# Runs of four channels instead of two in the spectra buffers of a long convolution

## Chip, cores and metric

The kernel runs on one core of a Trainium2 chip. The time is that of the device for one execution, in microseconds (us); lower is better.

## The reference

The input `u` has 2048 positions of 640 channels. Two branches work on it and a gate mixes them for each position:

```python
g = sigmoid((x * gate_w).sum(-1, keepdims=True))
# branch A: a state space layer as a long convolution, for each channel
K = 2.0 * einsum("dn,dnl->dl", C, exp(A * dt * pos)).real        # 640 x 2048 taps
y = irfft(rfft(u_t, 4096) * rfft(K, 4096), 4096)[..., :2048]     # causal convolution
a = y.T + u * D_skip
# branch B: feed-forward, 640 -> 1728 -> 640
b = maximum(x @ w1, 0) @ w2
out = g * a + (1 - g) * b
```

## The kernel before

The kernel has three kinds of work. The taps of the convolution are generated from the parameters in the first 405 us or so (tiles `pg`, `px`, `pk`, `sc`, `mg`, `G`, `kt`). The feed-forward branch goes through the hidden dimension in three passes of 5, 5 and 4 slices and keeps the partial sums in DRAM (tiles `pf`, `xx`, `w1h`, `w1l`, `w2h`, `w2l`, `hh`, `hl`, `q`). The convolution itself, in `conv`, runs from about 409 us, beside the third feed-forward pass, whose matmuls fill TensorE between its own.

The convolution is done by Fourier transforms in two factors, as matmuls with tables, for five blocks `i` of 128 channels. For each block:

1. `stage1`: the kernel's taps (`ck`) and the signal (`xu`) are multiplied with the table `tf` into a PSUM tile `pc`; each of four steps `q` covers 32 channels. VectorE then transposes the tile in blocks of 32x32 (`turn`, two instructions for a tile) into the spectra buffer `ku`. The output is addressed by `blocks`.
2. `stage2`: for each of eight groups `j` of four frequencies, matmuls with the table `tm` read kernel and signal spectra of one frequency for all 128 channels from `ku` (one moving operand of 2x128 columns). ScalarE copies one product from PSUM to `ku` (`copy`), VectorE makes two complex products (`mul`, into `kx` and into `ku`), and GpSimd adds and subtracts (`add`).
3. `inv2`: matmuls with the table `tn` read `ku`, again one frequency and 128 channels at a time; ScalarE copies the sums back (`back`).
4. `relay`: VectorE transposes eight pieces from the one half of `ku` to the other.
5. `inv1`: matmuls with `tw` read four frequencies of 128 channels (512 columns); ScalarE scales by the gate into `yo`, and the result goes out, or to a sum with the other branch.

One `ku` buffer holds, for each partition, kernel and signal spectra: 2 x 32 frequencies x 128 channels in float32. There are two such buffers. Within a half, channel `d` and frequency `g` lie at element 64·(d div 2) + 2·g + (d mod 2): channels in runs of two, and the frequencies of such a pair side by side.

The PSUM tiles `pc` come from a ring of three, and TensorE's queue is executed in order. The order of all instructions is made when the program is built: each step is a task with an engine, a duration estimate, a rank and the buffers it takes (`Plan.add`), and `Plan.run` lists the tasks by modelled due times. All engine calls go through one helper, so that the profile shows them all at line 408; they are told apart by their tiles.

Of the kernel before, what the change touches and what calls it, by code (L numbers as in the profile page):

```python
# [429 lines left out]
class Kernel:  # L430
# [850 lines left out]
    def conv(self, C=128):  # L1281
# [7 lines left out]
        st = {}  # L1289
# [8 lines left out]
        def table(k, shape, src):  # L1298
            def go():
                st[k] = self.pr.tile(shape, F32, name=k)  # L1300
                D_.dma_start(st[k], io[src])
            return A('SP', 'tab', 0.62, go, [opened], kb=math.prod(shape) * 4 / 1024, rank=3)
# [30 lines left out]


        def blocks(x, d0):
            return x[:, :, d0 // 2:d0 // 2 + 8].rearrange("p g e f -> p e f g")

        def stage1(kind, i, q, src):
            s_, ld = src
            b_ = tok('psc')  # L1340
            k = kind == 'k'
            if k and q == 0:
                K[i] = tok('K')
            buf = K[i]

            def pe():
                x = st['ck', i, q] if k else st['cu', i]
                p = st['p1', kind, i, q] = self.psc.tile([128, 2, 512], F32, name="pc")
                for c in range(2):
                    for h in range(2):  # L1350
                        r, o, d = slice(h * 64, h * 64 + 64), slice(c * 64, c * 64 + 64), slice(q * 32, q * 32 + 32)
                        self.E.matmul(p[o, h], st['tf'][r, int(k), o], x[r] if k else x[r, :, d], start=True, stop=True)

            def turn(h):
                def go():
                    if k and q == 0 and h == 0:
                        t = self.pr.tile([128, 2, 32, C], F32, name="ku", bufs=2)
                        st['ku', i] = t.rearrange("p k a b -> p k (a b)").rearrange("p k (e g f) -> p k g e f", g=32, f=2)
                        st['K', i], st['U', i] = st['ku', i][:, 0], st['ku', i][:, 1]
                    p = st['p1', kind, i, q]  # L1360
                    if k:
                        pv, d0 = p[:, h].rearrange("p (d b) -> p d b", b=32), h * 64 + q * 16
                    else:
                        pv, d0 = p.rearrange("p h (b d) -> p d h b", d=32)[:, 16 * h:16 * h + 16], q * 32 + h * 16
                    V.transpose(out=blocks(st['K' if k else 'U', i], d0), in_=pv)
                return go
            new = k and q == 0
            a = A('PE', 's' + kind, 0.87, pe, [ld, tf, opened] + ([] if k else [first[i]]), take=[b_, buf] if new else [b_], use=[s_] if new else [s_, buf],
                  rank=SKR if k else SUR, mode='c')
            pes[kind, i, q] = a  # L1370
            if JS1 and q % 2:
                self.plan.join([pes[kind, i, q - 1], a])
            ts = [A('DVE', 's' + kind, 0.68, turn(h), [a], use=[b_, buf], rank=SKD if k else SUD)
                  for h in range(2)]
            if new:
                first[i] = ts[0]
            return ts
# [3 lines left out]
        def stage2(i, j, dep):  # L1381
            b_, x_ = tok('psc'), tok('kx')

            def pe():
                ps = self.psc.tile([128, 2, 4, C], F32, name="pc")
                for a in range(2):
                    for m in range(4):
                        for p in range(2):
                            r, g = slice(p * 64, p * 64 + 64), 4 * j + m
                            self.E.matmul(ps[32 * m:32 * m + 32, p, 2 * a:2 * a + 2].rearrange("q k (e f) -> q k e f", f=2),  # L1390
                                          st['tm'][r, g, 32 * a:32 * a + 32], st['ku', i][r, :, g], start=True, stop=True)
                st['p2', i, j] = ps.rearrange("q p (a k) (e f) -> q k a p e f", a=2, f=2)

            def copy():
                S.copy(whole(i, j), st['p2', i, j][:, 0])

            def mul(a):
                def go():
                    k = whole(i, j)
                    if a:  # L1400
                        st['kx', i, j] = self.pr.tile([128, 2, 2, C], F32, name="kx", bufs=KX).rearrange(
                            "q b p (e f) -> q b p e f", f=2)
                    V.tensor_mul(st['kx', i, j] if a else k,
                                 st['p2', i, j][:, 1, None, a].to_broadcast([128, 2, 2, C // 2, 2]), k)
                return go

            def add(k):
                def go():
                    y, x = whole(i, j)[:, k], st['kx', i, j][:, 1 - k]
                    (P.tensor_add if k else P.tensor_sub)(y, y, x)  # L1410
                return go
            f = A('PE', None, 0.92, pe, dep, take=[b_], use=[K[i]], rank=S2P, mode='c', n=32)
            c = [A('ACT', 's2', 0.52, copy, [f], use=[b_, K[i]], rank=0.5)]
            for a in (1, 0):
                c.append(A('DVE', 's2', 0.62, mul(a), c, take=[x_] if a else (), use=[b_, K[i]] + [x_] * (1 - a), rank=S2D))
            return f, [A('POOL', 's2', 0.7, add(k), c, use=[x_, K[i]], rank=1) for k in range(2)]


        def whole(i, j):
            return st['K', i][:, 4 * j:4 * j + 4].rearrange("q (b p) e f -> q b p e f", b=2)  # L1420


        def inv2(i, h, dep):
            bs = tok('psc'), tok('psc')

            def pe(gs):
                if 0 in gs:
                    st['p3', i, h] = [self.psc.tile([128, 2, 4, C], F32, name="pc") for _ in range(2)]
                px = st['p3', i, h]
                for g in gs:  # L1430
                    for q in range(2):
                        for m in range(4):
                            for p in range(2):
                                r = slice(32 * m, 32 * m + 32)
                                self.E.matmul(px[m // 2][p * 64:p * 64 + 64, m % 2, g].rearrange("q (e f) -> q e f", f=2),
                                              st['tn'][r, 4 * h + g, p, q],
                                              whole(i, 4 * h + g)[r, q, p], start=q == 0, stop=q == 1)

            def back(k):
                def go():  # L1440
                    S.copy(st['U', i][:, 16 * h:16 * h + 16].rearrange("q (g m) e f -> q m g e f", m=4)[:, 2 * k:2 * k + 2],
                           st['p3', i, h][k].rearrange("q m g (e f) -> q m g e f", f=2))
                return go
            vs = []
            for t in range(TURNS):
                gs = range(t * 4 // TURNS, (t + 1) * 4 // TURNS)
                vs.append(A('PE', None, 1.85 / TURNS, lambda gs=gs: pe(gs), [*dep, tn] + vs[-1:], take=() if t else bs,
                            use=[K[i]] + (list(bs) if t else []), rank=S2P, mode='c', n=128 // TURNS))
            v = vs[-1]
            return vs, [A('ACT', 's2', 0.96, back(k), [v], use=[bs[k], K[i]], rank=0) for k in range(2)]  # L1450


        def relay(i, r, dep):
            return A('DVE', 'rl', 0.7, lambda: V.transpose(out=blocks(st['K', i], r * 16), in_=blocks(st['U', i], r * 16)),
                     dep, use=[K[i]], rank=RLR)
# [4 lines left out]
        def inv1(i, j, dep):  # L1460
            last = i == n - 1
            for q in range(2):
# [8 lines left out]
                def pe(q=q, b0=b0):  # L1471
                    py = st['p4', i, b0] = self.psc.tile([128, 2, 4, C], F32, name="pc")
                    for h in range(2):
                        self.E.matmul(py[h * 64:h * 64 + 64, 0].rearrange("q b (e f) -> q b e f", f=2), st['tw'],
                                      st['K', i][:, h * 16 + b0:h * 16 + b0 + 4], start=True, stop=True)

                def copy(q=q, b0=b0, ns=ns, y_=y_, first=first):
# [7 lines left out]
                a = A('PE', 's4', 0.87, pe, [*dep, tw], take=[b_], use=[K[i]], rank=S4R, mode='c1')  # L1485
# [49 lines left out]
        tm, tw, tn = table('tm', [128, 32, 64], 't_m'), table('tw', [128, 64], 't_w'), table('tn', [128, 8, 2, 2, 64], 't_n')  # L1535
# [69 lines left out]
```

## Time and profile before

| | us |
|---|---|
| median of 3 runs | 658.9 (657.89 to 659.11) |
| profiled execution | 659.89 |
| its span | 658.1 |

The mean granted TensorE clock of the profiled execution was 0.991 of full speed. In the lines of the profile PE is TensorE's matmul, PEld its weight load, DVE is VectorE, ACT ScalarE, POOL GpSimd, SP the queue of DMA issues. In a line of the tile view, the three numbers are minimum, median and maximum of one instruction in ns. In the lines of the timeline, the first two numbers are start and length in us, and the bracket holds the idle time of the engine before it and what ended it. In the view by stretches, the columns are the stretch, its length, the busy time of the engine (number of instructions), the granted clock, the share of DMA and GB/s. A matmul in float32 appears as two records with the same shape, so that `x1280` are 640 matmuls of the program.

### The profile page before, as it was taken

Reading aid. Unit: us, or ns where it says so; the run is one execution under the profiler, and the core shown is the slowest. Engines: PE = TensorE matmul, PEld = TensorE weight load, DVE = VectorE, ACT = ScalarE, POOL = GpSimd, SP = SyncE. Lnnn points to the kernel's source line nnn. Section 1 sums busy time; section 2 is a strip of 40 time slices with the busy share of each in tenths; the row PEclk is TensorE's granted clock in tenths of the full one; section 3 lists DMA queues with packets and bytes.
Section 4 is the critical chain, followed back from the end, with each engine's and each line's share of the span. In section 5 each row is a group of like instructions: output and inputs, shape, how many; then the busy total and the mean of one; then the engine's idle time right before and its main releaser. Section 6 shows DMA issues by size and latency. Waiting matters only on the chain. (4 is left out here: it accounts for less than half of the span.)

```text
span 658.1 us, 19202 instructions
## 1 busy us (share of the span) xinstructions
PE 637.3 (97%) x8236; PEld 509.0 (77%) x8236; DVE 510.2 (78%) x778; ACT 404.0 (61%) x603; POOL 96.6 (15%) x133
## 2 busy tenths in 40 slices
PE   7999999999999999999999999998997989999996
PEld 6999999899978988988988987645574445476576
DVE  4899838989999989999999995675677647685442
ACT  5467459998999888789889780051442343413531
POOL 0000000000000000000000000060430632712741
PEclk9999999999999999999999999999899999999999
DMA  9946855324575334432532359935417665264635
GB/s 262 316 186 196 271 146 167 108 74 154 147 233 174 121 116 152 153 113 79 207 124 77 97 151 297 287 89 117 145 56 212 123 177 107 49 227 141 181 90 129
DMA packets 76302, 102.79 MB, mean 156 GB/s; under 512 B 7609, under 2 KB 59449, under 8 KB 75962
## 3 DMA queue, kind: packets, MB, share of 16 engines
q1 hardware_dynamic: 76058, 101.16, 51.0%
q8 instruction: 65, 1.06, 0.7%
q10 hardware_dynamic: 160, 0.41, 0.3%
q14 instruction: 19, 0.16, 0.1%
HBM read 62.36 MB, written 39.19 MB: 154 GB/s over the span
## 5 line engine op out<-in xcount | busy, mean ns | idle before, releaser
L408 PE MATMUL pf<-xx,w1h 128*128 128x256 f32 (+1 forms) x760 | 187.4, 343 | 0.8 <-issue 0.4
L408 PEld LDWEIGHTS pf<-xx,w1h 128*128 128x128 f32 x760 | 125.7, 191 | 33.3 <-issue 18.9
L408 PE MATMUL pf<-xx,w1l 128*128 128x512 f32 (+1 forms) x340 | 116.6, 343 | 0.0
L408 ACT COPY ku<-pc 128x512 f32<-128x512 f32 (+1 forms) x60 | 44.5, 760 | 81.9 <-PE pc L408 81.7
L408 PE MATMUL pf<-w2h,hh 128*128 128x320 f32 x288 | 89.9, 316 | 0.4 <-ACT hh L408 0.4
L408 PE MATMUL pf<-w2l,hh 128*128 128x320 f32 x288 | 87.9, 309 | 0.0
L408 PE MATMUL pf<-w2h,hl 128*128 128x320 f32 x256 | 73.6, 313 | 0.0
L408 PEld LDWEIGHTS pf<-xx,w1l 128*128 128x128 f32 x340 | 65.0, 191 | 7.7 <-DVE w1l L408 0.2
L408 POOL TENSOR_TENSOR ku<-ku,kx 128x256 f32<-128x256 f32 x80 | 59.3, 776 | 65.2 <-PE pc L408 56.3
L408 DVE STREAM_TRANSPOSE ku<-pc 128x512 f32<-128x512 f32 x80 | 51.0, 689 | 22.8 <-PE pc L408 22.4
L408 POOL TENSOR_TENSOR kt<-kt,dsk 128x8 f32<-128x8 f32 x20 | 9.6, 480 | 392.0 <-DVE kt L408 275.5
L408 PEld LDWEIGHTS pf<-w2h,hh 128*128 128x128 f32 x288 | 54.2, 188 | 7.7 <-issue 6.2
L408 ACT ACTIVATE hh<-pf 128x512 fp32r<-128x512 f32 (+1 forms) x40 | 20.4, 510 | 57.7 <-PE pf L408 57.7
L408 PEld LDWEIGHTS pf<-w2l,hh 128*128 128x128 f32 x288 | 54.3, 188 | 0.6
L408 DVE TENSOR_TENSOR sc<-pg,sc 128x1024 f32<-128x1024 f32 x40 | 48.7, 1218 | 7.4 <-ACT sc L408 7.2
L408 ACT ACT_TABLE_LOAD x42 | 53.9, 1283 | 0.8
L408 ACT CAST sc<-pg 128x1024 int32<-128x1024 f32 x40 | 40.4, 1011 | 21.0 <-PE pg L408 20.9
L408 PE MATMUL pc<-ku,tm 64*32 64x256 f32 x1280 | 50.9, 456 | 0.2 <-DVE ku L408 0.2
L408 PEld LDWEIGHTS pf<-w2h,hl 128*128 128x128 f32 x256 | 46.5, 188 | 5.2 <-issue 4.6
L408 DVE TENSOR_TENSOR mg<-mg,sc 128x1024 f32<-128x1024 f32 x40 | 48.9, 1222 | 1.5
L408 DVE TENSOR_TENSOR sc<-sc,me 128x1024 f32<-128x1024 f32 x40 | 48.7, 1217 | 0.0
L408 ACT ACTIVATE sc<-sc,half_pi 128x1024 f32<-128x1024 f32 x40 | 45.7, 1142 | 0.0
(168 smaller groups left out, 1249.8 us busy)
## 6 DMA issues: line engine op xcount, KB each, us to landing
xx<-xt SPq DMA_DIRECT2D x24, 640.0 KB, 5.8
xt<-xx SPq DMA_DIRECT2D x16, 640.0 KB, 3.6
part<-q SPq DMA_DIRECT2D x16, 640.0 KB, 3.4
q<-part SPq DMA_DIRECT2D x16, 640.0 KB, 4.9
ws<-in_B_w_dram SPq DMA_DIRECT2D x20, 320.0 KB, 4.7
kd<-kt SPq DMA_DIRECT2D x80, 64.0 KB, 2.2
ck<-kd SPq DMA_DIRECT2D x40, 128.0 KB, 2.8
xu<-in_A_u_dram SPq DMA_DIRECT2D x10, 512.0 KB, 6.4
```

What stands on the lines that cost most here:

```text
L408: return lambda *a, **k: self._tc.keep_in_program_order(f(*a, **k))
```

## The change

The spectra buffer gets another layout: channel `d` and frequency `g` now lie at element 128·(d div 4) + 4·g + (d mod 4). Runs of four channels lie side by side, and behind them those of the next frequency. All views of the buffer are changed to it; the PSUM tiles keep their layout, since there only the names of the dimensions change. The tables, the DMAs and the number of instructions stay as they are, and so does the order in which the instructions stand on each engine. What changes in an instruction are its strides: a matmul that read 64 runs of two floats, 256 bytes apart, reads 32 runs of four, 512 bytes apart; a transpose that wrote the 32 frequencies of a channel in steps of 8 bytes writes them in steps of 16 bytes.

```diff
         def blocks(x, d0):
-            return x[:, :, d0 // 2:d0 // 2 + 8].rearrange("p g e f -> p e f g")
+            return x[:, :, d0 // 4:d0 // 4 + 4].rearrange("p g e f -> p e f g")
...
-                        st['ku', i] = t.rearrange("p k a b -> p k (a b)").rearrange("p k (e g f) -> p k g e f", g=32, f=2)
+                        st['ku', i] = t.rearrange("p k a b -> p k (a b)").rearrange("p k (e g f) -> p k g e f", g=32, f=4)
...
-                            self.E.matmul(ps[32 * m:32 * m + 32, p, 2 * a:2 * a + 2].rearrange("q k (e f) -> q k e f", f=2),
+                            self.E.matmul(ps[32 * m:32 * m + 32, p, 2 * a:2 * a + 2].rearrange("q k (e f) -> q k e f", f=4),
                                           st['tm'][r, g, 32 * a:32 * a + 32], st['ku', i][r, :, g], start=True, stop=True)
-                st['p2', i, j] = ps.rearrange("q p (a k) (e f) -> q k a p e f", a=2, f=2)
+                st['p2', i, j] = ps.rearrange("q p (a k) (e f) -> q k a p e f", a=2, f=4)
...
                         st['kx', i, j] = self.pr.tile([128, 2, 2, C], F32, name="kx", bufs=KX).rearrange(
-                            "q b p (e f) -> q b p e f", f=2)
+                            "q b p (e f) -> q b p e f", f=4)
                     V.tensor_mul(st['kx', i, j] if a else k,
-                                 st['p2', i, j][:, 1, None, a].to_broadcast([128, 2, 2, C // 2, 2]), k)
+                                 st['p2', i, j][:, 1, None, a].to_broadcast([128, 2, 2, C // 4, 4]), k)
```

In the same way `f=2` becomes `f=4` in the views of the matmuls of `inv2` and `inv1` and of the copy `back`.

More of the change, by code (lines that the diff above doesn't have):

```diff
@@ L1434, in pe @@
                                 r = slice(32 * m, 32 * m + 32)
-                                self.E.matmul(px[m // 2][p * 64:p * 64 + 64, m % 2, g].rearrange("q (e f) -> q e f", f=2),
+                                self.E.matmul(px[m // 2][p * 64:p * 64 + 64, m % 2, g].rearrange("q (e f) -> q e f", f=4),
                                               st['tn'][r, 4 * h + g, p, q],
@@ L1441, in go @@
                     S.copy(st['U', i][:, 16 * h:16 * h + 16].rearrange("q (g m) e f -> q m g e f", m=4)[:, 2 * k:2 * k + 2],
-                           st['p3', i, h][k].rearrange("q m g (e f) -> q m g e f", f=2))
+                           st['p3', i, h][k].rearrange("q m g (e f) -> q m g e f", f=4))
                 return go
@@ L1473, in pe @@
                     for h in range(2):
-                        self.E.matmul(py[h * 64:h * 64 + 64, 0].rearrange("q b (e f) -> q b e f", f=2), st['tw'],
+                        self.E.matmul(py[h * 64:h * 64 + 64, 0].rearrange("q b (e f) -> q b e f", f=4), st['tw'],
                                       st['K', i][:, h * 16 + b0:h * 16 + b0 + 4], start=True, stop=True)
```

## The prediction

> **What bounds the kernel now.** I read the page's busy times first, then the matmuls and vector operations that touch the spectra buffer, then the convolution stage in order of time.
>
> ```profile
> PE 637.3 (97%) x8236; PEld 509.0 (77%) x8236; DVE 510.2 (78%) x778; ACT 404.0 (61%) x603; POOL 96.6 (15%) x133
> PE 17%; DMA 2%; ACT 1%; SPq 1%; DVE 1%; issue 1%; POOL 0%; POOLq 0%; DVEq 0%; ACTq 0%
> ```
>
> TensorE is busy for 97% of the span, and it carries nearly all of the chain that ended last. VectorE comes second with 78%. The change touches only the operations on the buffer `ku`, which the view of that tile gives as minimum, median and maximum of one instruction:
>
> ```profile
> L408 PE MATMUL pc<-ku,tm x1280: 435/451/632, 428.2 to 614.9; 64*32 64x256 f32 x183
> L408 PE MATMUL pc<-ku,tn x1280: 265/307/466, 453.6 to 625.9; 32*64 32x128 f32 x183
> L408 DVE STREAM_TRANSPOSE ku<-pc x80: 666/678/740, 410.2 to 594.8; 128x512 f32<-128x512 f32 x80
> L408 PE MATMUL pc<-ku,tw x80: 589/591/1116, 486.3 to 638.3; 128*64 128x512 f32 x80
> L408 DVE TENSOR_TENSOR kx<-pc,ku x40: 669/687/699, 430.4 to 616.5; 128x512 f32<-128x512 f32 x40
> L408 DVE TENSOR_TENSOR ku<-pc,ku x40: 683/697/847, 431.1 to 617.2; 128x512 f32<-128x512 f32 x40
> L408 DVE STREAM_TRANSPOSE ku<-ku x40: 657/672/823, 465.5 to 633.8; 128x512 f32<-128x512 f32 x40
> ```
>
> They lie between 410 and 638 us. The number of instructions, their order on each engine and their waits are the same before and after. So everything hangs on whether one instruction takes longer or shorter with its new addresses. Two groups of addresses change in kind.
>
> **The matmuls: runs of two floats become runs of four.** Two other groups show what a matmul costs whose moving operand lies in runs of 512 and 64:
>
> ```profile
> L408 PE MATMUL pc<-ck,tf x160: 589/589/641, 409.1 to 581.5; 64*64 64x512 f32 x160
> L408 PE MATMUL pk<-mg,sc x1280: 216/219/243, 114.9 to 401.6; 128*32 128x64 f32 x183
> ```
>
> From 64 columns (219 ns) to 512 (589 ns) a column costs 370/448 = 0.83 ns. On that line 256 columns should take 378 ns and 128 columns 272 ns. The `tm` matmuls take 451, 73 more, and the `tn` matmuls 307, 35 more: in both, about 0.55 ns for each run of two. The `tw` matmuls also read runs of two and take 591 ns, on the line. They have two tiles of the array in flight; `tm` and `tn` have eight. My reading is that eight streams together ask for new places in the buffer faster than they are served: one run of two in 256x0.83/128 + 0.57 = 2.2 ns. A run of four has 3.3 ns before its next piece is due, so the wait should go. Eight matmuls run side by side, so 1280 of a kind are 160 in a row: 160x73 = 11.7 us for `tm` and 160x35 = 5.6 us for `tn`. Bounds: no gain (it is the eight tiles, not the runs) and 17.3 us.
>
> What of it is on the path is seen in one block's stage 2:
>
> ```profile
> 558.47 0.70 DVE L408 TENSOR_TENSOR kx<-pc,ku 128x512 f32<-128x512 f32 x1 [1.50 <-ACT ku L408]
> ...
> 569.68 0.82 DVE L408 TENSOR_TENSOR ku<-pc,ku 128x512 f32<-128x512 f32 x1
> ...
> 606.62 0.69 DVE L408 TENSOR_TENSOR kx<-pc,ku 128x512 f32<-128x512 f32 x1 [2.08 <-ACT ku L408]
> ```
>
> VectorE's sixteen products of this block go from 558.47 to 570.50, 12.0 us, of which 16x0.69 = 11.0 are its own work. If TensorE gets faster here, VectorE takes over after 1.0 us of the block's 11.7/5 = 2.3. In the last block, where feed-forward matmuls stand between (606.62, with 2.08 us of idle time on VectorE before one product), all 2.3 can come through. Four blocks at up to 1.0 and one at 2.3 make 6.3 at most; I take 5 of the 11.7 us. The `tn` matmuls wait for no VectorE work while they run: all 5.6. Together 10 us, if the reading is right. The products, ScalarE's copies and GpSimd's sums keep runs within a piece of the buffer and get longer ones; a product that writes in runs of two takes 697 ns, one that writes without a gap 687, so nothing is to be won there, and I put them at nothing. They would cost 10 ns x 40 = 0.4 us if that cover were wrong.
>
> **The transposes: a step of 8 bytes becomes one of 16.** A transpose writes, for each channel, 32 frequencies one behind the other; in the buffer these stand 8 bytes apart now and 16 after. The relay (`ku<-ku`) also reads in that step. No row of this profile shows VectorE at a step of 16 bytes in the same memory, so I bound it.
>
> ```profile
> L408 DVE TENSOR_TENSOR sc<-pg,sc 128x1024 f32<-128x1024 f32 x40 | 48.7, 1218 | 7.4 <-ACT sc L408 7.2
> 424.09 1.95 PE L408 MATMUL pc<-ck,tf 64*64 64x512 f32 x16
> 425.25 2.51 DVE L408 STREAM_TRANSPOSE ku<-pc 128x512 f32<-128x512 f32 x4 [2.57 <-PE pc L408]
> ...
> 545.94 1.90 PE L408 MATMUL pc<-xu,tf 64*64 64x512 f32 x16
> ...
> 552.68 2.47 DVE L408 STREAM_TRANSPOSE ku<-pc 128x512 f32<-128x512 f32 x4
> ```
>
> From below: nothing. The four transposes at 425.25 empty the matmuls of 424.09 and read kernel spectra that lie gapless in PSUM; the four at 552.68 empty those of 545.94 and read signal spectra in steps of 128 bytes there; both kinds take 0.62 us each. From above: VectorE passes an element in (1218-687)/512 = 1.04 ns, so at 8 bytes it moves to a new pair every 2.07 ns, and the 2.2 ns of the matmuls is the price of a new piece when it is asked for too fast. No row shows SBUF serving one stream at one new piece per 1.04 ns. At 2.07 ns for each element a transpose takes 512x2.07 + 90 ns = 1.15 us, 0.53 more. I exclude a gain: 0.62 us is 512x1.04 + 90 ns, the rate of the gapless products. I take the upper end, since the rows that are nearest in kind (same buffer, same memory) are the matmuls that pay for jumps, while the free row reads PSUM.
>
> The Trainium skill (Advanced Engine Details and Errata, section SBUF Cachelines) says that an access pattern runs at full rate only when at least two accesses in a row fall into the same line of 16 bytes. By it the transposes lose and the matmuls, with two floats to a line already, gain nothing; the trace speaks against the second half, with 451 ns where 378 would be full rate.
>
> **What 0.53 us x 120 does to the end.** VectorE by stretches, busy time and instructions:
>
> ```profile
> 410.00:430.00 20.00, 12.83 (x21) 1.00 0.95 285
> 443.00:465.00 22.00, 11.09 (x19) 0.93 0.45 98
> 465.00:486.00 21.00, 17.48 (x27) 0.99 0.39 144
> 486.00:516.00 30.00, 17.52 (x30) 0.94 0.68 166
> 534.00:558.00 24.00, 16.93 (x27) 1.00 0.60 138
> 574.00:598.00 24.00, 17.70 (x29) 1.00 0.55 188
> 628.00:635.00 7.00, 6.06 (x10) 1.00 0.43 129
> ```
>
> They hold 16, 16, 8, 24, 24, 24 and 8 transposes, so 8.5, 8.5, 4.2, 12.7, 12.7, 12.7 and 4.2 us more work: 63.6. If all idle time of a stretch could take it up, 1.3, 0, 0.7, 0.2, 5.6, 6.4 and 3.3 would be left: 17.5 us. But TensorE has three PSUM buffers there, its queue is in order, and it cannot catch up. The second stretch shows how much gets through:
>
> ```profile
> 440.71 1.95 PE L408 MATMUL pc<-ck,tf 64*64 64x512 f32 x16
> 443.00 2.50 DVE L408 STREAM_TRANSPOSE ku<-pc 128x512 f32<-128x512 f32 x4
> 444.17 1.09 PE L408 MATMUL pc<-xu,tf 64*64 64x512 f32 x8
> 445.08 1.11 PE L408 MATMUL pc<-ck,tf 64*64 64x512 f32 x8
> 445.42 0.66 DVE L408 SCALAR_TENSOR_TENSOR hl<-pf,hh 128x512 fp32r<-128x512 f32 x1
> 445.94 1.11 PE L408 MATMUL pc<-xu,tf 64*64 64x512 f32 x8
> 445.99 7.44 DVE L408 STREAM_TRANSPOSE ku<-pc 128x512 f32<-128x512 f32 x12
> 448.56 1.09 PE L408 MATMUL pc<-ck,tf 64*64 64x512 f32 x8
> 449.47 1.90 PE L408 MATMUL pc<-xu,tf 64*64 64x512 f32 x16
> 453.58 2.58 PE L408 MATMUL pc<-ku,tn 32*64 32x128 f32 x128
> ```
>
> Eight matmul records fill one buffer, and two transposes empty it, in 2.3 us then. From 443.0 the buffers come free at 445.3, 447.6, (after `hl`) 450.5, 452.8, 455.1, 457.4, 459.7. Each fill needs the buffer three before it: the fifth starts at 447.6 (now 445.9), the sixth at 450.5, the seventh at 452.8 (now 449.5), the eighth at 455.1. Then come 2.3 us of feed-forward, and `tn` takes two buffers, the seventh's at 459.7: 6.1 us later than now, of 8.5 added, though this stretch has 10.9 us of idle time behind the burst. So the loss lies well above the lower bound. I take the middle of 17.5 and 63.6, 40 us; the ends stay for the range. What is late next in each block is the first `tm` matmul, which needs all sixteen transposes, and `tw`, which needs all eight relays; the feed-forward matmuls queued behind them on TensorE wait too.
>
> **Sum.** The profiled execution took 659.9 us (span 658.1 and 1.8 around it), 1.0 above the median of 658.9. 659.9 + 40 - 10 = 689.9, less 1.0: **689 us**. Its own range goes from 666 (the lower bound, 17.5 us) to 704 (55 of the 63.6 lost).
>
> **Rivals.** Two per mille, 1.3 us, is about what a measurement of this kernel can tell from no change.
> - *Faster: the transposes stay at 0.62 us and the matmuls gain.* For it: 128-byte steps in PSUM are free. Against it: PSUM is not the memory written. It decides as soon as the loss per transpose is under 10/(40/0.53) = 0.13 us. 659.9 - 10 - 1 = 649 us (642 if all 17.3 come through). Chance 0.20.
> - *Only the transposes pay.* The excess of `tm` and `tn` comes from eight tiles in flight and stays; for it speaks `tw`, which reads the same runs for free. 659.9 + 40 - 1 = 699 us. Chance 0.17. This is how the page's two accesses to a line would have it.
> - *Half the price.* A transpose takes some 0.27 us more; added work 32 us, bounds 1.4 (what idle time leaves) and 32, middle 17; 17 - 10 = 7 more: 666 us. Chance 0.13.
> - *Nothing moves.* Both step and run are free: 659 us. Chance 0.08.
> The forecast, both effects, has 0.42.
>
> **Range and chances.** From 648 to 704: it leaves out the faster half-case below 648 (0.05) and the upper part of the transposes-only case and of the forecast (0.12). Faster by over 0.2%: 0.20 from the first rival and 0.02 from the half price: 0.22. Within 0.2%: 0.08. Slower: 0.70.
>
> **What would show it.** In the tile view after: `ku<-pc` and `ku<-ku` transposes near 1.15 us (right), near 0.68 (wrong, first or last rival), or between. `tm` near 378 and `tn` near 272 ns, or 451 and 307. In the waits, this line must grow to tens of us:
>
> ```profile
> PE pc L408 <- DVE ku L408: 0.2, 1, 0.2
> ```
>  If the transposes double and that idle time stays under 15 us, my coupling over three buffers is wrong.

## The result, and the profile after

The changed kernel takes 668.65 us (median of 4 runs, 667.65 to 673.05) against 659.0 before: 1.0164 times as long, 95% interval 1.0135 to 1.0192. On a second occasion it was 667.4 us, 1.0152 times (1.0129 to 1.0174). It is slower, as forecast, but by 9.7 us and not by 30. The execution that was profiled took 673.05 us (span 671.3) and is the longest of the four. So times of single instructions are read from it here, and differences of the whole from the medians.

The page's busy times after:

```profile
PE 630.2 (94%) x8236; PEld 508.0 (76%) x8236; DVE 546.6 (81%) x778; ACT 402.4 (60%) x603; POOL 92.2 (14%) x133
```

TensorE has 7.1 us less work, VectorE 36.4 us more. The view of the tile `ku` after (minimum, median, maximum of one instruction in ns) says where:

```profile
L408 PE MATMUL pc<-ku,tm x1280: 372/376/632, 431.5 to 622.8; 64*32 64x256 f32 x183
L408 PE MATMUL pc<-ku,tn x1280: 267/268/472, 458.1 to 636.4; 32*64 32x128 f32 x183
L408 DVE STREAM_TRANSPOSE ku<-pc x80: 1053/1101/1195, 410.3 to 604.7; 128x512 f32<-128x512 f32 x80
L408 POOL TENSOR_TENSOR ku<-ku,kx x80: 709/727/758, 435.0 to 628.6; 128x256 f32<-128x256 f32 x80
L408 PE MATMUL pc<-ku,tw x80: 592/592/643, 490.1 to 651.1; 128*64 128x512 f32 x80
L408 DVE TENSOR_TENSOR ku<-pc,ku x40: 681/692/694, 434.1 to 625.3; 128x512 f32<-128x512 f32 x40
L408 DVE STREAM_TRANSPOSE ku<-ku x40: 1057/1118/1206, 470.0 to 646.9; 128x512 f32<-128x512 f32 x40
```

`tm` fell from 451 to 376 ns, `tn` from 307 to 268; each transpose rose from some 675 to 1101 and 1118 ns. Both effects of the forecast are there. But the timeline of VectorE after shows that a row of transposes runs faster than single ones would suggest:

```profile
444.70 3.87 DVE L408 STREAM_TRANSPOSE ku<-pc 128x512 f32<-128x512 f32 x4
448.42 0.67 DVE L408 SCALAR_TENSOR_TENSOR hl<-pf,hh 128x512 fp32r<-128x512 f32 x1
449.01 11.20 DVE L408 STREAM_TRANSPOSE ku<-pc 128x512 f32<-128x512 f32 x12
```

Twelve in 11.20 us are 0.93 us each, where twelve took 7.44 before, 0.62 each: 0.31 us more, not 0.53. One is recorded as 1.10 us long, so the next transpose starts while the one before is still recorded as running. The waits of TensorE from 408 us on (total, times, longest, in us) have a new first line, the one named in the prediction, which had 0.2 us before:

```profile
PE pc L408 <- DVE ku L408: 17.5, 19, 3.0
PE pc L408 <- issue: 5.1, 4, 2.5
PE pc L408 <- ACT yo L408: 2.6, 2, 2.5
```

### The profile page after: what moved, and what is told of

Same layout as the page of the kernel before. It is cut to its first block, busy times and chain, and to the rows that moved or that the text cites. A ratio compares the mean times of both kernels' runs of the same rounds, so it can differ in the third digit from the quotient of the medians.

```text
span 671.3 us, 19202 instructions
## 1 busy us (share of the span) xinstructions
PE 630.2 (94%) x8236; PEld 508.0 (76%) x8236; DVE 546.6 (81%) x778; ACT 402.4 (60%) x603; POOL 92.2 (14%) x133
## 5 line engine op out<-in xcount | busy, mean ns | idle before, releaser
L408 DVE STREAM_TRANSPOSE ku<-pc 128x512 f32<-128x512 f32 x80 | 78.1, 1108 | 17.1 <-PE pc L408 17.1
L408 ACT COPY ku<-pc 128x512 f32<-128x512 f32 (+1 forms) x60 | 42.6, 730 | 79.1 <-PE pc L408 79.0
L408 POOL TENSOR_TENSOR ku<-ku,kx 128x256 f32<-128x256 f32 x80 | 55.5, 730 | 69.2 <-DVE ku L408 39.6
L408 DVE STREAM_TRANSPOSE ku<-ku 128x512 f32<-128x512 f32 x40 | 41.7, 1123 | 13.3 <-issue 9.3
```

Of the source, the lines that this page charges most:

```text
L408: return lambda *a, **k: self._tc.keep_in_program_order(f(*a, **k))
```

## The experiments

**The step of 16 bytes without long runs.** Kernel and signal spectra share one area, so that transposes step by 16 bytes and matmuls still read runs of two:

```diff
-  st['ku', i] = t.rearrange("p k a b -> p k (a b)").rearrange("p k (e g f) -> p k g e f", g=32, f=2)
+  st['ku', i] = t.rearrange("p k a b -> p (k a b)").rearrange("p (e g k f) -> p k g e f", g=32, k=2, f=2)
```

> Runs of two as before, but kernel and signal spectra share one area: element 128*(d div 2) + 4*g + 2*(kernel or signal) + (d mod 2). So the transposes step by 16 bytes, as in the changed kernel, while every matmul reads runs of two, 512 bytes apart. Theory 1 (the loss is the transposes' step, the gain the matmuls' run length): transposes 1.10 us and 0.93 back to back, tm 451 and tn 307 ns, time 659 + 20 = 679 us (672 to 684). Theory 2 (the loss is not the transposes', but the idle time of TensorE for instruction fetch and its clock): transposes slow, time 661 to 666. Theory 3 (what helps the matmuls is the distance of 512 bytes between runs, not their length): tm 376, tn 268, time near 669.

673.26 us, 1.0215 times the kernel before (1.0196 to 1.0233). The tile view of this kernel:

```profile
L408 PE MATMUL pc<-ku,tm x1280: 372/373/633, 431.1 to 624.7; 64*32 64x256 f32 x183
L408 PE MATMUL pc<-ku,tn x1280: 264/267/471, 457.8 to 636.6; 32*64 32x128 f32 x183
L408 DVE STREAM_TRANSPOSE ku<-pc x80: 1035/1082/1247, 409.9 to 606.6; 128x512 f32<-128x512 f32 x80
L408 PE MATMUL pc<-ku,tw x80: 680/727/1112, 490.0 to 651.4; 128*64 128x512 f32 x80
```

This throws over my reading of the matmuls: with runs of two, `tm` and `tn` are as fast as with runs of four. The matmuls' times are those of theory 3. The time lies in the range of theory 1, but not for its reason: `tw`, which never paid before, now takes 727 ns. Two `tw` run side by side, so by an estimate 80 of them lose 40x(727-592) = 5.4 us against the changed kernel, which is about what this kernel is slower than it (673.3 against 667.4, measured on the same occasion).

**Products alone in runs of four.** The spectra stay as before; only the products of stage 2 are stored in runs of four, in groups of other frequencies so that they fit into the place they free:

```diff
-  r, g = slice(p * 64, p * 64 + 64), 4 * j + m
+  r, g = slice(p * 64, p * 64 + 64), 16 * (m // 2) + 2 * j + m % 2
...
-  return st['K', i][:, 4 * j:4 * j + 4].rearrange("q (b p) e f -> q b p e f", b=2)
+  k = st['k4', i].rearrange("q (e s j f) -> q j s e f", s=4, j=8, f=4)[:, j]
+  return k.rearrange("q (b p) e f -> q b p e f", b=2)
```

> Spectra in runs of two as before, so all transposes and tm are as before; only the products of stage 2 are written in runs of four, into the place of the spectra that they use up (groups of frequencies 2j, 2j+1, 2j+16, 2j+17 in place of 4j to 4j+3, with the table of the inverse rearranged to match). Theory 1: transposes 0.68 us, tm 451, tn 268 ns instead of 307: 160 x 39 ns = 6 us less on TensorE's path, time 653 us (651 to 656). Rival (what tn gains is lost to a wait for ScalarE's copies behind it): 657 to 659.

655.91 us, 0.9963 times (0.9942 to 0.9984): 2 us gained. `tn` is at 268 ns and all transposes at 0.67 us:

```profile
L408 PE MATMUL pc<-ku,tm x1280: 440/452/633, 427.9 to 613.1; 64*32 64x256 f32 x183
L408 PE MATMUL pc<-ku,tn x1280: 264/268/470, 453.4 to 623.8; 32*64 32x128 f32 x183
```

Of the 6 us by which `tn` gets shorter about 2 reach the end. The prediction had let all of it through, and so had theory 1 here, with 653 us.

**Only the first transposes at 16 bytes.** Behind `tn` the buffer is used in runs of two again (copy back, relay, `tw`):

```diff
+        def late(i, k):
+            f = ((2,) * 5, (2,) * 5)[k][i]
+            return st['flat', i][:, k].rearrange("p (e g f) -> p g e f", g=32, f=f)
...
-  V.transpose(out=blocks(st['K', i], r * 16), in_=blocks(st['U', i], r * 16))
+  V.transpose(out=blocks(late(i, 0), r * 16), in_=blocks(late(i, 1), r * 16))
```

> The changed kernel, but behind the inverse's first matmuls (copy back, relay, last matmuls) the buffer is used in runs of two again: the 40 relays step by 8 bytes, the 80 first transposes by 16. Theory 1: relays 0.67 us, 40 x 0.32 = 13 us less on VectorE, of which half comes through: 668.7 - 6 = 662 us (658 to 666). Rival (the relays' loss is hidden, all of it comes from the first transposes): 667 to 669.

657.64 us, 0.9991 times (0.9973 to 1.0009): level with the kernel before. The relays are back near their old time, the first transposes are not:

```profile
L408 DVE STREAM_TRANSPOSE ku<-pc x80: 1048/1085/1185, 411.0 to 596.2; 128x512 f32<-128x512 f32 x80
L408 DVE STREAM_TRANSPOSE ku<-ku x40: 665/684/714, 469.5 to 633.4; 128x512 f32<-128x512 f32 x40
```

That is just under the expected range. It is 9.8 us better, where 6 were expected, than the changed kernel, which was run once more on the same occasion:

> The changed kernel once more, on the same chip as the others: 667 to 670 us, 1.3 to 1.9% over the kernel before.

(667.4 us, as given above.) So a third of the transposes, the relays, carries more than half of the loss (17.5 us, worked out below).

**The matmuls' gain alone.** The first experiment left another cause: which addresses the matmuls that run side by side read at the same time. Before, the four frequencies of a `tm` step lie 8 bytes apart, two of them in each 16 bytes. Here the layout is that of before, and only the frequencies that go together are others (the table of the inverse and the copy `back` are rearranged to match):

```diff
-  r, g = slice(p * 64, p * 64 + 64), 4 * j + m
+  r, g = slice(p * 64, p * 64 + 64), j + 8 * m
...
-  return st['K', i][:, 4 * j:4 * j + 4].rearrange("q (b p) e f -> q b p e f", b=2)
+  return st['K', i].rearrange("q (b p j) e f -> q j b p e f", b=2, j=8)[:, j]
```

> Layout as before, runs of two, all transposes at 8 bytes. Only the frequencies that one step of stage 2 takes together are others: j, j+8, j+16, j+24 (64 bytes apart) instead of 4j to 4j+3 (8 bytes apart), and so are the places of the products; the table of the inverse is rearranged to match. Theory 4 (what slows tm and tn is that streams that run side by side read from the same 16 bytes; the length of the runs has no part in it): tm 373, tn 267 ns, and since no transpose is slower, the gain of the matmuls alone: 5 to 10 us, 649 to 654 us. Theory 1 (the length of the runs): tm 451, tn 307, time as before, 658 us.

649.93 us, 0.9879 times (0.9861 to 0.9898): 8 us faster than before. The tile view:

```profile
L408 PE MATMUL pc<-ku,tm x1280: 372/373/632, 428.0 to 603.6; 64*32 64x256 f32 x183
L408 PE MATMUL pc<-ku,tn x1280: 264/267/471, 452.2 to 615.1; 32*64 32x128 f32 x183
L408 DVE STREAM_TRANSPOSE ku<-pc x80: 668/676/720, 410.0 to 585.3; 128x512 f32<-128x512 f32 x80
L408 DVE STREAM_TRANSPOSE ku<-ku x40: 669/675/718, 464.4 to 622.9; 128x512 f32<-128x512 f32 x40
```

The matmuls have their whole gain at runs of two and no transpose pays. The runs are 256 bytes apart, as before, so the 512 bytes of theory 3 in the first experiment are not the cause either. This version, called the spread version below, beats both kernels. It isn't free: of ScalarE's copies into `ku`, the 40 of 512 elements take 663 ns in the mean where they took 605. Repeated:

> The version with spread frequencies once more, on the same chip: 648 to 652 us, 1.0 to 1.4% under the kernel before.

651.34 us, 0.9906 times (0.9881 to 0.993): 6.5 us faster.

**Reading or writing.** The changed kernel with `late` as above, but with runs that differ by block (the first bracket is the half that is written, the second the half that is read, with one number for each block):

```diff
+  f = ((2, 2, 4, 4, 2), (4, 4, 2, 2, 2))[k][i]
```

> The changed kernel with three kinds of relays: blocks 0 and 1 read in steps of 16 bytes and write in steps of 8, blocks 2 and 3 read at 8 and write at 16, block 4 does both at 8. If the writing costs: blocks 0, 1 and 4 near 0.67 us, 2 and 3 near 1.1. If the reading costs: 0 and 1 near 1.1. If either is enough: 0 to 3 near 1.1.

669.21 us (one run). The relays in VectorE's timeline; the first row belongs to block 0, the second to block 1, the third to block 2, the last to block 4:

```profile
483.18 6.11 DVE L408 STREAM_TRANSPOSE ku<-ku 128x512 f32<-128x512 f32 x6
...
491.51 7.28 DVE L408 STREAM_TRANSPOSE ku<-ku 128x512 f32<-128x512 f32 x7
...
552.01 5.74 DVE L408 STREAM_TRANSPOSE ku<-ku 128x512 f32<-128x512 f32 x6
...
638.80 2.48 DVE L408 STREAM_TRANSPOSE ku<-ku 128x512 f32<-128x512 f32 x4
```

Reading at 16 bytes alone costs 1.02 to 1.04 us each, writing alone 0.96, neither 0.62. Either side is enough, and both together (1.02 in the changed kernel: 7 in 7.13 us) cost no more than reading alone.

**A step of 32 bytes.** Runs of eight, `f=8` in all views.

> The changed kernel with runs of eight: transposes step by 32 bytes, matmuls read runs of 32 bytes. If a transpose pays once for each new line of 16 bytes, 32 bytes cost what 16 do: 1.09 us and 0.93 back to back, time near 668. If it pays by distance, more: 1.3 us and over, time over 675. Matmuls as with runs of four, 376 and 268.

675.70 us (one run). VectorE's timeline:

```profile
449.23 11.66 DVE L408 STREAM_TRANSPOSE ku<-pc 128x512 f32<-128x512 f32 x12
```

0.97 us each, against 0.93 at 16 bytes: going from 8 bytes to 16 is what costs, the further distance hardly (between 8 and 16 nothing was tried). The time of the whole lies above the 668 us expected for that, where distance was to bring it. VectorE's busy time, 551.1 us against 546.6, is only 4.5 longer; one run doesn't settle the rest.

**Which addresses collide.** The interleaved layout with the frequencies of the spread version, which are 128 bytes apart there, so that the first and the third stream of `tm` are 256 apart:

```diff
-  r, g = slice(p * 64, p * 64 + 64), 4 * j + m
+  r, g = slice(p * 64, p * 64 + 64), j + 8 * m
```

> The interleaved layout (runs of two, frequencies 16 bytes apart) with frequencies j, j+8, j+16, j+24 side by side, 128 bytes apart. If streams collide only within 16 bytes: tm 373. If places 256 bytes apart collide too, which would also explain the tw of the interleaved layout (727 ns; its two streams are 256 bytes apart): tm 430 or more, tn (128 bytes apart) 267, tw 727 as there.

680.62 us (one run):

```profile
L408 PE MATMUL pc<-ku,tm x1280: 433/450/625, 431.2 to 632.4; 64*32 64x256 f32 x183
L408 PE MATMUL pc<-ku,tn x1280: 264/267/322, 459.2 to 643.6; 32*64 32x128 f32 x183
L408 PE MATMUL pc<-ku,tw x80: 680/733/1055, 492.9 to 658.4; 128*64 128x512 f32 x80
```

`tm` is slow again. The next table has, for the kernels so far and the one of the last experiment, the distance in bytes between neighbouring streams that read the same partitions, and the median in ns:

| kernel | `tm` | | `tn` | | `tw` | |
|---|---|---|---|---|---|---|
| before | 8 | 451 | 8 | 307 | 128 | 591 |
| after (runs of four) | 16 | 376 | 16 | 268 | 256 | 592 |
| interleaved | 16 | 373 | 16 | 267 | 256 | 727 |
| products in runs of four | 8 and 128 | 452 | 128 | 268 | 128 | 591 |
| only the first transposes at 16 bytes | 16 | 376 | 16 | 268 | 128 | 591 |
| spread | 64 | 373 | 64 | 267 | 128 | 591 |
| runs of eight | 32 | 376 | 32 | 268 | 512 | 593 |
| interleaved and spread | 128, so also 256 | 450 | 128 | 267 | 256 | 733 |
| spread, relays at 16 bytes (runs of four in `tw`) | 64 | 373 | 64 | 267 | 256 | 592 |

Every slow entry has streams within the same 16 bytes or 256 bytes apart; entries at 16, 32, 64 and 128 bytes are fast. At 256 bytes the length of the runs does count: `tw` takes 727 ns with runs of two (interleaved) and 592 with runs of four (changed kernel), with the same distance of streams and of runs. That the memory has banks of 16 bytes that repeat every 256 fits the slow entries, but is a reading. Why runs of four at 256 bytes, and of eight at 512, escape was not tried; streams with longer runs ask for a new place less often, which would fit.

**Only the relays at 16 bytes**, in the spread version (runs of four in `late`):

> The version with spread frequencies, but behind the inverse's first matmuls the buffer is used in runs of four: only the 40 relays step by 16 bytes. If the relays cost the same here as in the changed kernel (9.8 us of its 17.5 us loss, although they are a third of the transposes): 649.9 + 9.8 = 660 us (657 to 662). If each transpose costs alike: 649.9 + 17.5/3 = 656 us.

659.63 us, 1.0025 times (1.0003 to 1.0047), 8.3 more than the spread version on the same occasion. The relays cost near the same here as in the changed kernel, where they were 9.8.

## Why the prediction was right in direction and wrong in size

**The step that failed** is the price of a transpose: 0.53 us more was put into the sum, 0.31 was measured. One transpose alone takes 1.10 us, close to the 1.15 that I had worked out, but what counts in a burst is the distance from one start to the next. Before, the row has 678 ns for one and the burst 0.62 us each: I used the burst's 0.62 as the base and put the price of an isolated piece on top, 2.07 ns for every element, where 0.93 us for 512 elements leaves (930-90)/512 = 1.64 ns. The upper bound became the value taken, and nothing in the rows stood between the ends. What had spoken for it were the matmuls that paid 2.2 ns for each new piece of the buffer; the spread version, where runs of two cost them nothing, shows that this was no price of a new piece.

With 0.31 the rest of the sum comes out. 120x0.31 = 37 us more work (VectorE's busy time rose by 36.4); per stretch 5.0, 5.0, 2.5, 7.4, 7.4, 7.4 and 2.5, of which its idle times leave 0, 0, 0, 0, 0.3, 1.1 and 1.6: a lower bound of 3, an upper of 37, the middle 20. 659.9 + 20 - 10 - 1.0 = 669, against 668.65. That it fits this closely is partly luck: the middle of the bounds was a guess, and by the differences of kernels below the two parts were 17.5 (or 16.1) where 20 stands and 8.4 (or 6.5) where 10 stands, so that their errors cancel.

**The coupling over three buffers** held in the stretch for which it had been worked out. In the second stretch, the same walk at 0.93 us gives a `tn` start 3.1 us late instead of 6.1. The timeline of TensorE after:

```profile
442.47 1.95 PE L408 MATMUL pc<-ck,tf 64*64 64x512 f32 x16
...
448.72 1.09 PE L408 MATMUL pc<-xu,tf 64*64 64x512 f32 x8 [0.66 <-DVE ku L408]
452.01 1.09 PE L408 MATMUL pc<-ck,tf 64*64 64x512 f32 x8 [0.61 <-issue]
452.89 1.09 PE L408 MATMUL pc<-xu,tf 64*64 64x512 f32 x8
454.81 1.09 PE L408 MATMUL pc<-xu,tf 64*64 64x512 f32 x8 [0.84 <-DVE ku L408]
458.10 2.41 PE L408 MATMUL pc<-ku,tn 32*64 32x128 f32 x128
```

From the first fill to `tn` it is 458.10-442.47 = 15.63 us, before 453.58-440.71 = 12.87: 2.8 us late, with waits for VectorE at the fifth and the eighth fill; the walk has them at the fifth, the seventh and the eighth. TensorE's waits for these transposes grew from 0.2 to 17.5 us, and to 14.9 in the profile of the repeated run, short of the tens that the prediction named with its higher price.

**The loss.** The changed kernel and the spread version differ only in the layout of four and the grouping of frequencies; `tm` and `tn` are alike in them (376 and 373, 268 and 267 ns). Their difference, 667.4-649.9 = 17.5 us (two occasions; 16.1 with the repeated spread version), is taken as the transposes' cost at the end: 47% of the work added. It leaves out that ScalarE's copies are longer in the spread version. Against the spread version, the kernel with only the relays at 16 bytes lies 8.3 us higher, the one with only the first transposes 7.7 (two occasions). VectorE's busy time is 509.3 us in the spread version, 522.9 and 532.5 in these two: 13.6 us more for the 40 relays, 23.2 for the 80 first transposes. So about 60% of the relays' added work reaches the end, and a third of the other. The forecast counted both kinds alike. My reading, which was not tested, is that relays are dearer since nothing of their block can go on beside them: `tw` needs all eight. In the last block, `tw` waits for them directly, in TensorE's timeline after:

```profile
648.06 3.65 PE L408 MATMUL pc<-ku,tw 128*64 128x512 f32 x16 [2.34 <-DVE ku L408]
```

**The gain.** The forecast of 378 and 272 ns for the matmuls held (376 and 268), that of 10 us on the path nearly (8.4 and 6.5 on the two occasions of the spread version); the reason did not. I had blamed the runs of two, since `tw` read them free with two tiles in flight and `tm` paid with eight. For `tm` and `tn` what differed was the distance of the streams; the length of the runs showed only in `tw` at 256 bytes. So the change's only gain needs no change of layout. Within the gain I had taken 5 us from `tm` and all 5.6 from `tn`; the products' kernel shows 2 from `tn`, so `tm` must have given most of the rest; that was not tried alone.

**Lines of 16 bytes.** The Trainium skill (Advanced Engine Details and Errata, section SBUF Cachelines) asks for two accesses in a row within a line of 16 bytes. For the transposes the trace agrees: 0.62 us at 8 bytes, 0.93 at 16, 0.97 at 32. I had held the trace against it for the matmuls, wrongly: runs of two read at full rate in the spread version (373 ns).

**The rivals.** The time fell nearest to "half the price" (666 us). "Faster" is out, since the transposes pay; "only the transposes pay" is out, since the matmuls gain; "nothing moves" is out on both counts. GpSimd's sums and ScalarE's copies, put at nothing, became some 5% shorter (GpSimd 773 to 727 ns), on engines that TensorE does not wait for much. One reading of the profile in the prediction was off, without bearing on the sum: the chain that ended last, as its line shows it, follows only some 23% of the span, 17% of it on TensorE, which is not nearly all of it.

## What to carry to other kernels

Price an instruction in a burst by the distance of starts, in the base and in the addition; a duration of one holds a part that overlaps the next. When matmuls in separate tiles of the array run side by side and are slower than their column count, look first at which addresses they read at the same time: regrouping them (here which four frequencies go together) cost only longer copies on ScalarE and gave 0.9 to 1.2%. For VectorE's transposes of float32, keep the innermost step in SBUF at 8 bytes, on the read and the write side; the steps of 128 bytes at which the signal spectra are read in PSUM cost nothing (0.62 us each, as without gaps).

## What was not expected of the hardware

In these kernels, matmuls that read the same partitions at the same time slow each other down by about a fifth when they read from the same 16 bytes (451 against 373 ns for 256 columns) or, with runs of two, from places 256 bytes apart (450 against 373, and 727 against 592 for 512 columns). A transpose at a step of 16 bytes holds VectorE for 1.5 times as long and not twice (0.93 against 0.62 us), whether the step is on the side that is read (1.02) or written (0.96), and 32 bytes cost little more (0.97).
